# Attention with a window and global keys, then a gated feed-forward: the whole kernel written as one list of small steps

## The chip, the cores and the metric

The kernel runs on one core of a Trainium2 chip. A core has five engines that run side by side: TensorE (PE, matrix products), VectorE (DVE), ScalarE (ACT), GpSimd (POOL) and SyncE (SP, which here only issues transfers); each takes its instructions in order. PE writes to PSUM, which has eight banks of 512 float32 per partition; DVE and ACT can read them. Transfers from and to the chip's memory are issued from SP, ACT or POOL and carried by 16 DMA engines that all queues share. The metric is the device time of one execution in microseconds (us), given as the median of the runs; lower is better.

## The reference

Four batches, eight heads, 768 positions, 64 elements a head. A query sees the 8 first keys and the 96 keys up to itself, with a bias that falls with the distance. The result, 3072 rows of 512, goes through a feed-forward (FF) with a gate.

```python
scores = scale * np.matmul(q, k.transpose(0, 1, 3, 2))
is_global = pos[None, :] < 8
is_local = (rel >= 0) & (rel < 96)
dist = np.where(is_global & ~is_local, 96.0, np.abs(rel))
scores = np.where(is_global | is_local, scores - slopes[:, None, None] * dist, -1e9)
a = np.exp(scores - max); a = a / (np.sum(a, axis=-1) + 1e-09)
x = np.matmul(a, v)                         # -> (3072, 512)
g = x @ w_gate                              # (512, 1536)
out = (g / (1 + np.exp(-g))) * (x @ w_val) @ w_out
```

## The kernel before

Everything on PE is float16 with float32 sums. Tokens are worked in tiles of 384 (half a batch, eight tiles in all). The parts:

**Scores.** Keys are cut into seven chunks of 120 (the last has 48); each chunk's 128 columns of `kT` hold the 8 global keys and then the chunk's own. A chunk meets the 216 queries that can see it. Two heads (a pair, `hp`) lie in the upper and lower 64 rows of `qT` and `kT`, so that their score products run side by side. Two or three chunks share one PSUM bank of 432 columns; one such bank pair for two heads is what `scores` (line 357) or `scores_half` (line 338) makes. ACT takes the exponential of each head's bank (lines 351 and 375), and DVE or POOL multiplies it by `masks`, the exponential of the biased distance (lines 355, 383, 386). In the first half of batch 0, and a part of the second, the bias is instead added on PE by `bias` (line 327): a matmul of `slopeI`, the scaled unit matrix, with `dist`.

**Values.** A `Quad` is four heads. `weigh` (line 436, matmuls at 443) makes the denominators (`den`, with a matrix of ones) or one half of the numerators (`num`); four heads with 32 columns each run side by side. `invert` and `spread` (lines 450 and 457) make reciprocals on DVE with two transposes of 32x32 blocks, and the numerators, copied by ACT to `ns` (line 474), are scaled into `xT` by POOL (line 478), for batch 0 by DVE (lines 478, 499).

**Feed-forward.** For a tile t and one of 12 blocks f of 128 hidden units, `products` (line 506) makes four gate and four value matmuls of 384 columns. ACT takes a tanh (`th`, line 527), DVE makes `sl` (line 529) and `hT` (line 533), which must read a gate sum and then a value sum. `out_part` (line 537) makes a quarter of an output row block, three matmuls of 512 columns; after four, ACT evicts (`osb`, line 559) and SP stores.

**Order.** It is written by hand. At the start come warming matmuls (`fill`, 28 in all), then for each pair of batch 0 the transposes of the first half, the scores, the sums. Batch 0's V is loaded for its first half in rows of three tokens (`v16`), and `p_perm` (line 595) puts the rows in their key chunks with 12 matmuls with a 0/1 matrix `perm` (line 598), evicted by ACT and DVE (line 601). Then `stretches` (line 726) mix FF groups with attention steps: after every FF group a share `quota` is added to `owed`, and when it reaches 1 the next attention step is put in. What a step leaves for DVE or POOL waits in `later`. Each gate group is followed at once by the value group of the same f, and each output part by its place in `outs`. Loads are tied to places in the FF (`at_step`, line 737). Batch 0, and half of batch 1, are transposed on PE; the rest by transposing DMAs from SP (`transposes_dma`, line 394), after which `spread_keys` (line 403) copies the keys into their chunks on DVE.

**PSUM.** Eight single banks: `a0` to `a3` in turn for scores, sums and transposes (`bank`, line 236), `x0` to `x2` in turn for gate and value sums, `o0` for outputs.

**Loads.** POOL issues the casting loads (float32 to float16), SP the constants, the first two pairs of q and k in float32, the copies of the global values (`copy_globals`, line 183), the transposing DMAs and the stores.

Of the kernel before, what the change touches and what calls it, by code (L numbers as in the profile page):

```python
# [15 lines left out]
KC = 120  # L16
WIN = 216
# [18 lines left out]

@with_exitstack
def kernel(
# [31 lines left out]
    const_dr = nc.inline_tensor(  # L70
        np.concatenate([np.eye(128, 160, dtype=np.float16), dist_np], axis=1), name="consts")
# [23 lines left out]


    consts = sb.tile([128, 160 + 3 * WIN], FP16, name="consts")
    nc.sync.dma_start(out=consts, in_=const_dr.ap())
    identx, ident, dist = consts[:, 0:160], consts[:, 0:128], consts[:, 160:]


    J2 = TB // 128
    q32 = sb2.tile([128, H // 2, J2 * D], FP32, name="q32", tag="qst")
    k32 = sb2.tile([128, H // 2, J2 * D], FP32, name="k32", tag="kst")
    q16 = sb2.tile([128, 2, H, J2 * D], FP16, name="q16", tag="qst")
    k16 = sb2.tile([128, 2, H, J2 * D], FP16, name="k16", tag="kst")
    v16 = sb.tile([128, H, J2 * D], FP16, name="v16")
    for hp in range(2):
        for st, src in ((k32, k), (q32, q)):
            nc.sync.dma_start(  # L110
                out=st[:, 2 * hp:2 * hp + 2, :],
                in_=src[0, 2 * hp:2 * hp + 2, 0:TB, :].rearrange(
                    "h (p j) d -> p h (j d)", p=128))

    def load_half(dst, src, half, h0, h1):
        nc.gpsimd.dma_start(
            out=dst, in_=src[0, h0:h1, TB * half:TB * half + TB, :].rearrange(
                "h (p j) d -> p h (j d)", p=128))

    vSs = [sb.tile([128, NCH, H, D], FP16, name=f"vS{b}") for b in range(B)]  # L120
    for b in range(1, B):
        nc.gpsimd.memset(vSs[b][:, 6, :, :], 0.0)
    load_half(v16, v, 0, 0, H)
    load_half(k16[:, 0, 4:8], k, 0, 4, 8)
    load_half(q16[:, 0, 4:8], q, 0, 4, 8)

    masks = sb.tile([128, H, 3 * WIN], FP16, name="masks")
    ones = sb.tile([128, 256], FP16, name="ones")
    nc.vector.memset(ones, 1.0)

    NC0 = 4
    perm = sb.tile([128, J2, NC0, 128], FP16, name="perm")
    nc.vector.memset(perm.rearrange("p j c m -> p (j c m)").bitcast(mybir.dt.uint32), 0)
    kTs = [sb.tile([128, NCH * 128], FP16, name=f"kT{i}") for i in range(NP)]

    vS3 = sb.tile([128, H, D], FP16, name="vCut")


    nc.vector.memset(vSs[0][:, 6, :, :], 0.0)
    for t in kTs:  # L140
        nc.vector.memset(t[:, 3 * 128 + NG + TB - 3 * KC:4 * 128], 0.0)
        nc.vector.memset(t[:, 6 * 128 + 56:], 0.0)
    for j in range(J2):
        nc.vector.tensor_copy(
            out=perm[:, j, :, NG + j::J2],
            in_=identx.rearrange("p (c m) -> p c m", c=NC0))
        n = (NG - j + J2 - 1) // J2
        nc.vector.tensor_copy(
            out=perm[:, j, :, j:NG:J2],
            in_=identx[:, 0:n].unsqueeze(1).broadcast_to([128, NC0, n]))  # L150

    slopeI = sb.tile([128, H, 128], FP16, name="slopeI")

    def make_slope(eng, h):
        eng(slopeI[:, h, :], ident, -slopes[h] / scale)

    qst, kst = {}, {}

    def stage(b):
        qst[b] = sb2.tile([128, H, J * D], FP16, name="qst", tag="qst")  # L160
        kst[b] = sb2.tile([128, H, J * D], FP16, name="kst", tag="kst")

    def load_qk(b, h0, h1):
        for st, src in ((kst[b], k), (qst[b], q)):
            nc.gpsimd.dma_start(
                out=st[:, h0:h1, :],
                in_=src[b, h0:h1].rearrange("h (p j) d -> p h (j d)", p=128))

    def load_v_rest(b, c):
        n = min(KC, S - KC * c)  # L170
        nc.gpsimd.dma_start(  # L171
            out=vSs[b][NG:NG + n, c, :, :],
            in_=v[b, :, KC * c:KC * c + n, :].rearrange("h p d -> p h d"))


    vG = sb.tile([NG, B, H, D], FP16, name="vG")

    def load_globals():
        nc.gpsimd.dma_start(
            out=vG.rearrange("p b h d -> p (b h) d"),  # L180
            in_=v[:, :, 0:NG, :].rearrange("b h p d -> p (b h) d"))

    def copy_globals(b):
        c0 = 3 if b == 0 else 0
        nc.sync.dma_start(
            out=vSs[b][0:NG, c0:, :, :],
            in_=vG[:, b, :, :].unsqueeze(1).broadcast_to([NG, NCH - c0, H, D]))


    def stage_rows(b):  # L190
        qst[b] = sb2.tile([128, NP, J, 2, D], FP16, name="qst", tag="qst")
        kst[b] = sb2.tile([128, NP, J, 2, D], FP16, name="kst", tag="kst")

    def rows_of(st, b, hp):

        if b > 1:
            return st[b][:, hp]
        return st[b][:, 2 * hp:2 * hp + 2, :].rearrange("p h x -> p (h x)").rearrange(
            "p (t e d) -> p t e d", t=J, e=2)

    def load_rows(b, i, h):
        st, src = ((qst, q), (kst, k))[i]
        nc.gpsimd.dma_start(  # L203
            out=rows_of(st, b, h // 2)[:, :, h % 2, :],
            in_=src[b, h].rearrange("(t p) d -> p t d", p=128))

    wg = sb.tile([128, NC, DFF], FP16, name="wg")
    wv = sb.tile([128, NC, DFF], FP16, name="wv")
    wo = sb.tile([128, NFF, DM], FP16, name="wo")
    WF = 512  # L210

    def load_w(n, g):
        f0 = WF * n
        for w, src in ((wg, moe_w_gate), (wv, moe_w_val)):
            nc.gpsimd.dma_start(
                out=w[:, 2 * g:2 * g + 2, f0:f0 + WF],
                in_=src[256 * g:256 * g + 256, f0:f0 + WF].rearrange("(p s) f -> p s f", s=2))

    def load_wo(g):
        nc.gpsimd.dma_start(  # L220
            out=wo[:, 4 * g:4 * g + 4, :],
            in_=moe_w_out[512 * g:512 * g + 512].rearrange("(f p) d -> p f d", p=128))


    xTs = {}
# [5 lines left out]

    state = {"tags": ["a0", "a1", "a2", "a3"], "n": 0, "x": ["x0", "x1", "x2"]}

    def bank(name, dt=FP32):
        tag = state["tags"][state["n"] % len(state["tags"])]
        state["n"] += 1
        return single(name, tag, dt)

    def banks(name, dt=FP32):
        return [bank(name, dt) for _ in range(2)]

    def single(name, tag, dt=FP32):
        return ps.tile([128, 512 if dt == FP32 else 1024], dt, name=name, tag=tag)


    def make_masks(h, c0, c1):
        nc.scalar.activation(
            out=masks[:, h, c0:c1], in_=dist[:, c0:c1], func=AF.Exp, scale=-slopes[h])  # L250

    later = []

    def run_later(n):
        for _ in range(n):
            if later:
                later.pop(0)()

    class Pair:
        def __init__(self, b, hp):  # L260
            self.b, self.hp = b, hp
            self.at = {}

        def transposes(self):
            b, hp = self.b, self.hp
            trq, trk = (t[:, 0:S] for t in banks("trs", FP16))
            for st, tr in ((kst[b], trk), (qst[b], trq)):
                for j in range(J):
                    for hi in range(2):
                        nc.tensor.transpose(  # L270
                            tr[64 * hi:64 * hi + 64, 128 * j:128 * j + 128],
                            st[:, 2 * hp + hi, D * j:D * j + D], ident)
            self.qT = sb2.tile([128, S], FP16, name="qT", tag="qT", bufs=NP)
            self.kT = kTs[hp]
            k3 = self.kT.rearrange("r (c m) -> r c m", m=128)
            t3 = trk.rearrange("r (j p) -> r p j", j=J)
            for c0, c1, n in ((0, 6, KC), (6, 7, S - 6 * KC)):
                nc.scalar.copy(
                    out=k3[:, c0:c1, NG:NG + n].rearrange("r c (p j) -> r c p j", j=J),
                    in_=t3[:, 20 * c0:20 * c0 + (c1 - c0) * (n // J), :].rearrange(  # L280
                        "r (c p) j -> r c p j", c=c1 - c0))
            nc.scalar.copy(
                out=self.qT.rearrange("r (p j) -> r p j", j=J),
                in_=trq.rearrange("r (j p) -> r p j", j=J))
            nc.vector.tensor_copy(
                out=k3[:, :, 0:NG],
                in_=k3[:, 0, NG:2 * NG].unsqueeze(1).broadcast_to([128, NCH, NG]))


        def transposes_half(self, half, tr, k_eng):  # L290
            hp = self.hp
            trq, trk = tr
            for st, dst in ((k16, trk), (q16, trq)):
# [542 lines left out]
```

## Time and profile before

| what | value |
|---|---|
| median of three runs | 253.75 us (252.83 to 256.88) |
| the profiled execution, first to last instruction (its span; the profile gives no other time of it) | 252.9 us |
| PE busy | 241.3 us, 95% |
| DVE, ACT, POOL busy | 168.7, 130.9, 105.0 us |
| mean granted TensorE clock | 0.998 |
| DMA | 25.63 MB in 86499 packets, of which 76288 under 512 bytes |
| the chain that ended last | PE 80%, DVE 8%, ACT 4%, DMA 3% |

Busy times are from the profile's first part, of one execution. A group of instructions is given with its count, its busy time and the mean duration of one; PE's matmuls overlap, so that the distance from one start to the next, not the duration, is what one costs in a row. The chain that ended last is followed back from the last instruction, at each step to what released it.

### The profile page before, as it was taken

How to read it: one execution, taken by the hardware profiler on the slowest of the kernel's cores; microseconds unless marked ns; L12 is line 12 of the kernel's file. 1: busy time of each engine (PE TensorE's matmuls, PEld its weight loads, DVE VectorE, ACT ScalarE, POOL GpSimd, SP SyncE). 2: the span in 40 equal slices, each digit the busy share in tenths (PEclk: the TensorE clock that was granted, in tenths of full speed). 3: DMA queues.
4: the chain of work that ended last, by engine and by line, in shares of the span. 5: the costliest groups of instructions: out<-in, count | busy, mean ns of one | idle time of the engine just before them, and what ended most of it. 6: DMA issues, size and time to landing. Idle time of an engine off the chain costs nothing.

```text
span 252.9 us, 5999 instructions
## 1 busy us (share of the span) xinstructions
PE 241.3 (95%) x2384; PEld 136.1 (54%) x2384; DVE 168.7 (67%) x379; ACT 130.9 (52%) x290; POOL 105.0 (42%) x123
## 2 busy tenths in 40 slices
PE   6997999899889999999999999999999999999994
PEld 4664556464435556555555555555555555555541
DVE  7365779856695666979785656978875666555510
ACT  3476787559464455464653653555735634332321
POOL 9663664550054975913609865803020232200000
PEclk9999999999999999999999999999999999999999
DMA  6999999991950999993916997991011101100122
GB/s 157 188 203 181 180 207 205 167 131 42 127 69 4 141 150 173 129 143 64 117 44 67 150 157 88 147 109 45 0 44 41 44 0 44 43 20 24 41 83 83
DMA packets 86499, 25.63 MB, mean 101 GB/s; under 512 B 76288, under 2 KB 83528, under 8 KB 86472
## 3 DMA queue, kind: packets, MB, share of 16 engines
q0 software_dynamic: 65408, 13.83, 65.7%
q1 hardware_dynamic: 20920, 11.30, 21.8%
q8 instruction: 18, 0.29, 0.5%
q10 hardware_dynamic: 144, 0.13, 0.2%
q14 instruction: 9, 0.07, 0.1%
HBM read 28.63 MB, written 6.29 MB: 138 GB/s over the span
## 4 chain that ended last, share of the span: by engine, by line
PE 80%; DVE 8%; ACT 4%; DMA 3%; SPq 2%; issue 1%; DVEq 0%; ACTq 0%
PE ops L545 23%; PE gps L516 22%; PE vps L516 22%; PE num L443 3%; PE sc L366 2%; PE den L443 2%; DVE sl L529 2%; DMA kN<-kst 2%; DMA q<-in_q_dram 2%; ACT at L351 1%; PE trs L296 1%; PE warm L574 1%; PE sc L343 1%; PE psv L598 1%; SPq L399 1%
## 5 line engine op out<-in xcount | busy, mean ns | idle before, releaser
L529 DVE SCALAR_TENSOR_TENSOR sl<-th,gps 128x384 f32<-128x384 f32 x94 | 51.8, 552 | 45.4 <-ACT th L527 44.3
L527 ACT ACTIVATE th<-gps 128x384 f32<-128x384 f32 x94 | 46.4, 494 | 63.1 <-PE gps L516 61.6
L516 PE MATMUL gps<-xT,wg 128*128 128x384 f16 x376 | 77.0, 326 | 0.7 <-DVE xT L478 0.6
L516 PE MATMUL vps<-xT,wv 128*128 128x384 f16 x376 | 76.5, 326 | 0.5 <-DVE sl L529 0.4
L545 PE MATMUL ops<-wo,hT 128*128 128x512 f16 x288 | 75.5, 379 | 0.0
L533 DVE TENSOR_TENSOR hT<-vps,sl 128x384 f16<-128x384 f32 x94 | 51.7, 550 | 7.2
L478 POOL TENSOR_TENSOR xT<-ns,rb 128x384 f16<-128x384 f32 x24 | 23.9, 1013 | 77.5 <-DVE rb L459 62.4
L516 PEld LDWEIGHTS <-wg 128*128 128x128 f16 x384 | 35.8, 98 | 33.1 <-issue 3.1
L516 PEld LDWEIGHTS <-wv 128*128 128x128 f16 x384 | 36.8, 98 | 26.4 <-issue 2.1
L545 PEld LDWEIGHTS <-hT 128*128 128x128 f16 x288 | 27.4, 98 | 25.1 <-issue 0.4
L375 ACT ACTIVATE at<-sc 128x432 f16<-128x432 f32 x72 | 33.6, 535 | 9.0 <-PE sc L366 9.0
L171 POOL DMA_DIRECT2D vS<-in_v_dram x25 | 22.3, 898 | 9.1 <-DMA k<-in_k_dram 3.4
L559 ACT ACTIVATE osb<-ops 128x512 f32<-128x512 f32 x23 | 13.7, 597 | 18.0 <-PE ops L545 18.0
L474 ACT COPY ns<-num 128x384 f32<-128x384 f32 x28 | 12.0, 482 | 12.7 <-PE num L443 11.9
L203 POOL DMA_DIRECT2D qst<-in_q_dram x20 | 16.8, 854 | 2.7 <-DMA wo<-in_moe_w_out_dram 1.6
L203 POOL DMA_DIRECT2D kst<-in_k_dram x20 | 17.0, 865 | 2.0 <-DMA wo<-in_moe_w_out_dram 1.1
L386 DVE TENSOR_TENSOR at<-at,masks 128x864 f16<-128x864 f16 x20 | 12.9, 645 | 4.4 <-ACT at L375 4.4
L351 ACT ACTIVATE at<-sc 128x432 f16<-128x432 f32 (+2 forms) x32 | 11.5, 447 | 5.1 <-PE sc L343 5.1
L386 POOL TENSOR_TENSOR at<-at,masks 128x864 f16<-128x864 f16 x4 | 7.3, 1821 | 13.6 <-ACT at L375 13.6
L443 PE MATMUL num<-at,vS 128*32 128x216 f16 (+6 forms) x560 | 12.0, 226 | 0.0
L443 PE MATMUL den<-at,ones 128*32 128x216 f16 (+6 forms) x288 | 9.4, 229 | 2.4 <-DVE at L383 1.8
L443 PEld LDWEIGHTS <-ones 128*32 128x32 f16 x288 | 5.7, 96 | 9.2 <-issue 8.9
(76 smaller groups left out, 176.1 us busy)
## 6 DMA issues: line engine op xcount, KB each, us to landing
out_dram<-osb SPq DMA_DIRECT2D x23, 256.0 KB, 2.0
vS<-in_v_dram POOLq DMA_DIRECT2D x21, 120.0 KB, 8.1
kst<-in_k_dram POOLq DMA_DIRECT2D x20, 96.0 KB, 4.9
qst<-in_q_dram POOLq DMA_DIRECT2D x20, 96.0 KB, 4.7
wg<-in_moe_w_gate_dram POOLq DMA_DIRECT2D x6, 256.0 KB, 8.6
wv<-in_moe_w_val_dram POOLq DMA_DIRECT2D x6, 256.0 KB, 9.6
wo<-in_moe_w_out_dram POOLq DMA_DIRECT2D x3, 512.0 KB, 11.1
k<-in_k_dram SPq DMA_DIRECT2D x2, 192.0 KB, 3.8
```

The lines of the kernel that those rows point to most:

```text
L171: nc.gpsimd.dma_start(out=vSs[b][NG:NG + n, c, :, :], in_=v[b, :, KC * c:KC * c + n, :].rearrange("h p d -> p h d"))
L203: nc.gpsimd.dma_start(out=rows_of(st, b, h // 2)[:, :, h % 2, :], in_=src[b, h].rearrange("(t p) d -> p t d", p=128))
L351: nc.scalar.activation(out=at[:, hi, 0:col + n], in_=sc[hi][:, 0:col + n], func=AF.Exp, scale=scale)
L375: nc.scalar.activation(out=at[:, hi, :], in_=sc[hi][:, 0:BANK], func=AF.Exp, scale=scale)
L386: mul_eng.tensor_mul(at, at, m[:, :, o:o + BANK])
L443: nc.tensor.matmul(dst[r, o:o + n], lhsT=ones[:, 0:32] if side is None else vals[:, 4 * g + j, side::2], rhs=pairs[b, 2 * g + j // 2].at[c ...
L478: mul_eng.tensor_mul(self.x_out(half, side), srcs[side], self.rb)
L516: nc.tensor.matmul(gv[f, which][:, 0:TB], lhsT=w[:, c, 128 * f:128 * f + 128], rhs=x_of(t)[:, c, :], start=(c == 0), stop=(c == NC - 1))
L527: nc.scalar.activation(out=th, in_=dst[:, 0:TB], func=AF.Tanh, scale=0.5)
L529: nc.vector.scalar_tensor_tensor(out=sl, in0=th, scalar=1.0, in1=dst[:, 0:TB], op0=AluOp.add, op1=AluOp.mult)
L533: nc.vector.tensor_mul(hTs[t][:, f, :], dst[:, 0:TB], gv["sl"])
L545: nc.tensor.matmul(ops, lhsT=hTs[t][:, f, 128 * i:128 * i + 128], rhs=wo[:, f, :], start=(f == 0), stop=(f == NFF - 1))
```

## The change

The kernel's helpers become functions of small steps, and one text, `ORDER`, names every step once, in the order in which it is recorded (1,091 steps; each engine takes its own in that order). There is no `stretches`, `quota`, `owed`, `later`, `at_step`; a word such as `c.1.2.0` is the scores of batch 1, pair 2, unit 0, and a last letter V, A or P names the engine where it is open.

- **Steps.** Gate group (`g`), tanh (`t`), `sl` (`s`), value group (`v`) and `hT` (`h`) are separate, as are the score matmuls (`c`), their exponential (`x`) and mask (`m`), denominators and the two halves of numerators (`w`), and so on. The f of a tile come in any order; `sl` has five buffers and `th` three (two each before); exponentials' tiles have one more.
- **PSUM.** Two doubles (two banks each, `S0` and `S1`, in turn) for a pair's scores and for both halves of numerators; four singles for gate, value, output, transposes and denominators. A single is dealt in the order in which the list frees them.
- **One instruction for two.** The exponential of a pair's two heads is one ACT instruction on a double (864 elements for two of 432), and so is the copy of both numerator halves.
- **V straight.** `v16`, `perm`, `p_perm` and its evictions are gone: all seven chunks of batch 0's V come by `Lv` loads in key chunks, like those of the other batches. V has three buffers for the four batches.
- **Loads.** They stand in the list at their own places. Before the first weights come the first halves of q and k, four V chunks and the second halves of q and k of four heads. The two first q loads issue from ACT. The loads of q and k of batches 1 to 3 stand much earlier than their use. The constants come as two loads.
- **Which engine.** 21 of 40 mask steps are POOL's (4 of 52 mask instructions before), 14 of 32 scalings of numerators (24 before). In batch 0's second half pairs 0 and 1 take the bias on PE, pairs 2 and 3 masks.
- **The end.** The last 128 rows' sums go to the two banks of a double, in 24 matmuls of 256 columns (12 of 512 before), so that ACT and DVE each evict a bank of their own.

The core of the diff:

```diff
+ORDER = """
+pre Z.0.P Li fill.2 Lh.0.0.4.8 sl.2 sl.4 LG Lh.1.0.4.8 Lf.A.1.0 sl.7 fill.14 sl.6 cast.1.0.V T.0.0.1
+Lf.S.0.0 Lf.A.1.1 sl.1 sl.0 cast.0.0.V T.0.0.0 cast.1.1.A Lf.S.0.1 Lv.0.2 T.1.0.1 cast.0.1.A T.1.0.0
+Ld.S M.5.1 k.0.0.V B.0.1 q.0.0.V c.0.0.1 x.0.0.1 sl.3 B.0.0 c.0.0.0 M.4.0 Lh.1.1.0.4 x.0.0.0 q.1.0.V
+Lv.0.0 k.1.0.V G.0.1.4.V B.1.0 c.0.1.0 sl.5 T.2.0.1 T.2.0.0 k.2.0.V x.0.1.0 B.1.1 c.0.1.1 x.0.1.1
+T.3.0.0 q.2.0.A T.3.0.1 B.2.1 B.2.0 c.0.2.1 x.0.2.1 c.0.2.0 x.0.2.0 w.0.0.0.0 q.3.0.V B.3.0 k.3.0.V
+c.0.3.0 T.0.1.1 Lv.0.1 Lv.0.3 w.0.0.0.1 w.0.0.0.2 Lh.0.1.0.4 x.0.3.0 B.3.1 q.0.1.A c.0.3.1 Lw.0.0.0
+T.0.1.0 i.0.0.0 x.0.3.1 w.0.1.0.0 r.0.0.0 p.0.0.0.0.V Lw.0.0.1 k.0.1.A Lw.1.0.0 p.0.0.0.1.V Lw.1.0.1
+Lh.0.1.4.8 w.0.1.0.1 w.0.1.0.2 Lh.1.1.4.8 M.7.0 i.0.1.0 r.0.1.0 B.0.2 c.0.0.2 Lw.0.1.1 M.6.0
+Lw.0.1.0 Lv.0.6 Lw.1.1.0 T.1.1.1 q.1.1.A T.1.1.0 p.0.1.0.0.V ga.0.0 ga.0.2 p.0.1.0.1.V k.1.1.A g.0.3
...
+"""
...
+    def double(name, dt=FP32):
+        tag = f"S{turn['s'] % 2}"
+        turn["s"] += 1
+        return ps.tile([128, 2, 512 if dt == FP32 else 1024], dt, name=name, tag=tag)
+    busy = {tag: None for tag in XT}
+    freed = list(XT)
+    def single(name, key, dt=FP32):
+        tag = freed.pop(0)
+        busy[key] = tag
+        return named(name, tag, dt)
+    def release(key):
+        freed.append(busy.pop(key))
...
+    def ld_v(b, c):
         n = min(KC, S - KC * c)
         nc.gpsimd.dma_start(
-            out=vSs[b][NG:NG + n, c, :, :],
+            out=v_of(b)[NG:NG + n, c, :, :],
             in_=v[b, :, KC * c:KC * c + n, :].rearrange("h p d -> p h d"))
...
+        nc.scalar.activation(
+            out=at[:, :, 0:w], in_=scs.pop((b, hp, u))[:, :, 0:w], func=AF.Exp, scale=scale)
...
+            if last_rows(t, i):
+                for e in range(2):
+                    c = slice(DM // 2 * e, DM // 2 * e + DM // 2)
+                    nc.tensor.matmul(ops[:, e, 0:DM // 2], lhsT=lhsT, rhs=wo[:, f, c],
+                                     start=(f == 0), stop=(f == NFF - 1))
...
-    def p_perm(c, eng):
-        psv = p_single("psv", "v")
-        for j in range(J2):
-            nc.tensor.matmul(
-                psv, lhsT=perm[:, j, c, :], rhs=v16[:, :, D * j:D * j + D],
-                start=(j == 0), stop=(j == J2 - 1))
...
+    for step in ORDER.split():
+        name, *args = step.split(".")
+        WORK[name](*(int(a) if a.isdigit() else a for a in args))
```

## The prediction

> **What bounds the kernel now.** I read the shares first, then the windows, then the chain of waits, then single stretches of the timeline.
>
> ```profile
> span 252.9 us, 5999 instructions
> PE 241.3 (95%) x2384; PEld 136.1 (54%) x2384; DVE 168.7 (67%) x379; ACT 130.9 (52%) x290; POOL 105.0 (42%) x123
> ...
> DMA  6999999991950999993916997991011101100122
> ```
>
> TensorE (PE) sets the time; every digit of the DMA row is one fortieth of the span, and the transfers are full up to about 57 us. But a busy PE is not PE at its peak. The chain of waits gives the pitch of matmuls that follow one another:
>
> ```profile
> 79.94 1.29 PE ops L545 x6
> 81.23 0.65 PE gps L516 x4
> ```
>
> Six matmuls of 512 columns take 1.29 us and four of 384 take 0.65: 0.42 ns a column. At that pitch the whole work is 192 groups x 0.65 = 124.8 (gate and value) + 288 x 0.215 = 61.9 (output) + 8.8 (scores, two heads side by side) + 13.2 (denominators and numerators, four side by side) + 2.9 (bias) + 3.9 (transposes) + 2.6 (V permutation) = 218. I call that the pipelined work; 35 us of the span are not that. Counting each window's matmuls at that pitch shows where they are.
>
> ```profile
> core 0: us, PE busy (x) PEld busy (x) DVE busy (x) ACT busy (x) POOL busy (x), PEclk, DMA share, GB/s
> 20.00:30.00 10.00, 8.93 (x117) 5.34 (x118) 7.80 (x19) 6.09 (x15) 4.38 (x6) 1.00 1.63 184
> 30.00:40.00 10.00, 9.58 (x154) 5.89 (x149) 7.34 (x20) 8.48 (x23) 6.47 (x9) 1.00 1.28 205
> 40.00:50.00 10.00, 9.15 (x114) 5.22 (x113) 8.84 (x19) 6.64 (x19) 4.41 (x6) 1.00 1.67 186
> 60.00:80.00 20.00, 17.86 (x193) 9.38 (x191) 15.23 (x36) 11.16 (x25) 4.60 (x5) 1.00 0.53 76
> 80.00:100.00 20.00, 20.00 (x234) 11.36 (x236) 13.25 (x28) 9.96 (x21) 15.80 (x20) 1.00 1.66 132
> ```
>
> In 20-30, for one, 16 + 12 gate and 8 value matmuls (0.1625 each) are 5.85, transposes, scores and sums 1.8: 7.65. So counted, the pipelined work is 1.4 in 0-10, 6.5 in 10-20, 23.5 in the 30 us from 20 to 50 (6.5 lost), 15.4 in 60-80 (4.6 lost), then 154 in the 160 us to 240 (6 lost); the end loses 4. So the loss is the start (12 us before the feed-forward, FF), the first FF tile beside batch 0's second half, and batch 1's first half.
>
> ```profile
> 10.90 1.29 PE psv L598 x6
> ...
> 13.09 1.40 PE psv L598 x6
> ...
> 23.29 0.81 PE gvps L516 x4
> ```
>
> The start is one chain through load, casts, scores, exponentials, denominators, with V's permutation (psv) in PE's order between them; the first gate product that continues comes at 22.8. In the trace the first weight blocks land at 13.5 to 18.2 us, the second at 25.0 to 28.9, the third at 33.4 to 37.2: the start is bound by order, not by weights.
>
> **The change part by part.** Sum against the execution of 252.9 us; the median of the runs is 253.75, 0.85 more.
>
> *Start.* V in key chunks takes away 12 psv matmuls (12 x 0.224 = 2.7 us on PE), four evictions (0.6 to 0.7 each) and 0.7 + 1.5 us of permutation building on DVE; fills fall from 28 to 16. Exponentials of two heads become one instruction: 535 ns at 432 and 323 at 168 elements give 0.8 ns an element over 0.19 fixed, so 0.88 for 864 in place of 0.95 for two in a row. V chunks cost 0.93 us of transfer each (landings at 29.87 and 30.83), four before the weights = 3.7, where the one load of V's half took 1.5; two half-1 loads of 1.0 to 1.4 also stand ahead of the weights. So 18.2 becomes about 22 for the value block and 18.5 to 19 for the gate block, which now goes first (wg before wv). Two q loads issue from ACT (0.5 each, before its table load), which SP no longer issues. DVE has 12 to 13 us to do from the first landing near 4, so x is ready at 17 to 19; the second numerators' double waits for DVE's first xT products inside that. The first gate starts near 19.5, not 22.8 (3.3), with 7.7 us of pipelined work behind it, not 6.0 without psv (1.7). Bounds: 0 if the loads are late by 4, 6 if they are as before. **-4.5.**
>
> *First FF tile.* The list keeps gate groups ahead of value groups (five sl buffers), and puts batch 0's half 1 into the weight gaps. From 10 to 31 us of PE work DVE has 41 instructions, 20.7 us at their pitch (two xT in 1.01); third-block weights land near 33 to 36 by the same landing steps (1.3 a block), when PE asks for them at about 32. DVE, 99% as long as PE's 21, is next: I take 24.5 us for these 21, 3.5 lost in place of 6.5. Bounds: nothing gained, or all but DVE's own 0.5. **-3.1.**
>
> *Batch 1.* The kst/qst of the first two head pairs land at 46.7 and 48.7 now; the new load order puts them ahead of part of wo, near 40 to 42. Transposes and scores then lie among tile 1's groups, with output parts kept back as cover. In 60-80 the chain runs through kN (DMA 4.3 us), kT and masks. I take 1.2 of 4.6 left; bounds 0 and 4.6. **-3.4.** The transposes share SP's queue with the output stores; a late transpose holds the store behind it, and with two osb buffers ACT's third eviction.
>
> *Later.* PSUM: doubles carry scores and numerators, four singles the rest. 21 masks move to POOL (1.82 each there, 0.61 on DVE), ten xT products from POOL (1.01) to DVE (0.55). Bias grows by 672 columns (+0.3). The last 128 rows go as 24 matmuls of 256 columns (fills at full pace: 0.127 each, 3.05 against 2.58, +0.5), and ACT and DVE then empty two banks together (-0.4). Cost of POOL's tensor work on DVE: the timeline has it.
>
> ```profile
> 65.19 0.17 DVE L410 COPY kT<-kN 128x48 f16<-128x48 f16 x1
> ...
> 69.28 2.12 POOL L478 TENSOR_TENSOR xT<-ns,rb 128x384 f16<-128x384 f32 x2 [15.11 <-ACT at L375]
> ...
> 69.48 0.98 DVE L410 COPY kT<-kN 128x48 f16<-128x48 f16 x1
> ...
> 70.46 1.40 DVE L386 TENSOR_TENSOR at<-at,masks 128x864 f16<-128x864 f16 x1
> ```
>
> The same copy takes 0.17 alone and 0.98 beside POOL, a mask 1.40 for 0.60. FF's own sl and hT do not change (552 ns both ways). Bounds 0 to 7; I take 0.9, since DVE has a third of its time free. **+1.3 in all.**
>
> Sum: -4.5 - 3.1 - 3.4 + 1.3 = -9.7; 252.9 - 9.7 = 243.2, as a median **244.0**.
>
> The busy share would allow less. PE idles 2.3 us in 20-50 and 2.1 in 60-80, so by that row the two middle terms could give at most 4.4, not 6.5, and the time would be 246. The Trainium skill ("Perfetto Trace Analysis", section "Identifying the Most-Contended Engine") says matmul busy share is a bad measure of headroom, because matmuls are pipelined; by that rule the time is 244, and this trace's pitches agree.
>
> **The rivals.**
> 1. *Transfers hold the start* (0.10): first FF no earlier than 22.8 and later blocks late too. For: DMA is full, and V's rows are now 256-byte runs. Against: the weights land 4 us before their use now. Start 0, first tile -2: 249.6, within 2%.
> 2. *POOL holds up DVE* (0.08): 35 tensor instructions, 52 us of POOL in some 180, meet 54 key copies and masks on DVE; 0.29 x 54 = 16 hits of 0.8 = 12.6 us of DVE. If half lies where DVE is the limit, +6.3 in place of 0.9: 249.4. The Trainium skill ("SBUF — State Buffer", section "Who interferes with whom") says that a DVE instruction with two SBUF inputs contends with GpSimd's reads and that 2-port copies are locked out whole; by that rule more POOL masks mean this case, and the two rows above agree.
> 3. *Singles run out* (0.12), slower: gate, value, output, denominator and transpose sums share four banks. An output part holds one for four parts; three banks turn in 3 x 0.65 = 1.95 us. A gate bank is held 0.65 + 0.49 + 0.55 = 1.69, and 2.57 when its tanh stands behind a merged exp of 0.88: 0.62 lost. 44 exps lie beside FF: 27 us if each hits. It makes the kernel slower from 24 of 44 (15 us); at two thirds, 262. Against: three banks serve gate and value now, exps come in pairs of 0.95, and 80-240 loses only 6 in 160.
>
> **How the numbers follow.** Forecast 0.70, rivals 0.10, 0.08, 0.12. A measurement here tells about 2% from no change, 248.7 to 258.8. Faster 0.72 (the forecast and the better edge of rivals 1 and 2), within 2% 0.16, slower 0.12. The range: all favourable bounds together (-6, -6, -4.6, +0.3) give 237; upward it takes in rivals 1 and 2: 238 to 252.
>
> **What would show it.** Right: psv gone, first gate before 21 us; windows from 22 to 80 with 9 or more us of pipelined work in 10; DVE over 80% in the first tile; steady part unchanged. Wrong: gate matmuls waiting for weight landings (1); masks and kT copies near 1 us on DVE with PE waiting for them (2); many gate groups in 80-240 ended by sl or th (3). PE idle over 3 us between 5 and 19 us would slow its matmuls (fills: 0.225 each at 6.7 us, 0.127 at 10) and cost 2 to 3.

## The result and the profile after

The changed kernel takes **264.04 us** (median of 4 runs, 262.62 to 266.10) against 253.38 (4 runs, 252.83 to 256.88) for the kernel before on the same chip: a ratio of **1.041, 95% interval 1.036 to 1.045**. It is slower, where 244.0 was forecast and 0.12 was given to slower. The execution in the profile took 266.1, with a span of 263.9. All ratios in this text leave out executions more than 1.5% above the fastest of their kernel (medians and ranges keep them), and the profiles of runs 1, 6 and 12 below are of such executions, so that what only they show is not settled.

The page of the changed kernel, with the row of the clock that TensorE was granted (each digit is a fortieth of the span, 6.6 us, in tenths of full speed):

```profile
span 263.9 us, 5821 instructions
PE 242.0 (92%) x2368; PEld 136.0 (52%) x2368; DVE 168.5 (64%) x364; ACT 119.6 (45%) x216; POOL 130.4 (49%) x142
...
PEclk9689999999779999999599999999999999999999
DMA  7999969999997999990152996610014011101212
```

The sums hardly moved: DVE is as busy as before, ACT 11 us less, POOL 25 us more. But the clock row, all nines before, has three dips, at 7 to 20, 66 to 79 and 125 to 132 us; and the DMA row has a dip at 33 to 40 and then hardly a rest up to 119, where the kernel before was quiet at 57 to 63 and at 70 to 82. The windows say which stretches lost time:

```profile
core 0: us, PE busy (x) PEld busy (x) DVE busy (x) ACT busy (x) POOL busy (x), PEclk, DMA share, GB/s
20.00:30.00 10.00, 10.00 (x127) 5.99 (x124) 8.51 (x21) 8.06 (x18) 5.74 (x10) 1.00 1.49 195
30.00:40.00 10.00, 9.89 (x158) 6.06 (x157) 9.33 (x19) 7.14 (x15) 9.14 (x12) 1.00 0.79 113
60.00:80.00 20.00, 13.80 (x133) 6.47 (x135) 10.33 (x27) 6.23 (x10) 11.23 (x13) 0.83 2.03 141
120.00:130.00 10.00, 5.17 (x20) 2.17 (x21) 7.23 (x8) 0.42 (x2) 4.65 (x4) 0.71 0.00 0
```

Read the matmul counts: 133 in 60-80 where there were 193, and 20 in 120-130. With each matmul at its pitch, as in the prediction, the time that is not pipelined work (fills and the V permutation left out of the work) is:

| stretch | before, lost us | after, lost us | change | forecast |
|---|---|---|---|---|
| to the first gate group (22.8; 20.56) | 16.15 | 13.38 | -2.8 | -4.5 |
| from there to 60 | 5.51 | 3.10 | -2.4 | -3.1 |
| 60 to 80 | 4.57 | 10.25 | +5.7 | -3.4 |
| 80 to 110 | 1.69 | 4.38 | +2.7 | the three: +1.3 |
| 110 to 130 | 1.07 | 8.15 | +7.1 | |
| 130 to the end | 7.50 | 7.93 | +0.4 | |

These add up to +10.7; with 0.3 more work that is the 11.0 between the two spans. So at 60 us the changed kernel is 5.2 us ahead, at 80 it has lost that, and 10 us more go by 130. The waits of PE (us in total, times, longest):

```profile
PE sc L471 <- DVE kT L437: 6.6, 2, 5.2
PE sc L471 <- DMA qT<-qst: 4.3, 1, 4.3
PE num L530 <- DMA vS<-in_v_dram: 2.5, 2, 1.5
```

POOL's timeline shows both of the causes that the runs below bear out:

```profile
29.76 2.61 POOL L498 TENSOR_TENSOR at<-at,masks 128x144 f16<-128x144 f16 x4 [2.31 <-ACT at L481]
33.23 1.82 POOL L498 TENSOR_TENSOR at<-at,masks 128x864 f16<-128x864 f16 x1 [0.86 <-ACT at L481]
34.99 0.81 POOL L289 DMA_DIRECT2D qst<-in_q_dram  x1
...
115.32 9.33 POOL L498 TENSOR_TENSOR at<-at,masks 128x864 f16<-128x864 f16 x7
```

**The stop near 120.** From 115.32 on POOL runs seven masks without a pause. DVE's timeline beside them:

```profile
117.06 0.56 DVE L592 TENSOR_TENSOR hT<-vps,sl 128x384 f16<-128x384 f32 x1 [0.28 <-PE vps L576]
117.53 5.45 DVE L434 COPY kT<-kN 128x720 f16<-128x720 f16 x1
122.91 1.78 DVE L436 COPY kT<-kN 128x48 f16<-128x48 f16 x1
```

A key copy that takes 0.34 us alone starts during the second mask and takes 5.45; the next, 0.17 alone, takes 1.78 and ends with the row. Everything on DVE waits behind them, and PE stands from 119.62 to 124.83.

**The stop near 68.** The first three lines of POOL's timeline: three mask steps of batch 0 stand ahead of batch 1's loads in its queue, and POOL issues no load between 26.74 and 34.99. The rest is in the chain that ended last (start, us, what):

```profile
54.77 8.76 DMA qst<-in_q_dram
...
63.67 7.87 DMA qT<-qst
...
75.16 1.28 PE ops L610 x3
...
78.33 1.29 PE ops L610 x6
```

The last rows of head 5's queries are issued at 54.77 and land at 63.53; their transposition takes another 7.87, and PE stands from 67.31 to 71.59. The last two lines are the same output matmuls: 0.43 us each after the stop, 0.215 three us later. After the stop at 120 nine of them take 4.05 us from 126.92 on (PE's timeline):

```profile
124.83 0.90 PE L471 MATMUL sc<-qT,kT 64*128 64x216 f16 x8 [5.21 <-DVE kT L437]
125.66 1.46 PE L576 MATMUL vps<-xT,wv 128*128 128x384 f16 x4
126.92 4.05 PE L610 MATMUL ops<-wo,hT 128*128 128x512 f16 x9
```

That is 2.1 more than at full pace; the scores and value matmuls ahead of them lost another 1. So these two stops cost their length and 2.5 to 3 us behind it.

### The profile page after: what moved, and what is told of

Same layout as the page of the kernel before. It is cut to its first block, busy times and chain, and to the rows that moved or that the text cites. A ratio compares the mean times of both kernels' runs of the same rounds, so it can differ in the third digit from the quotient of the medians.

```text
span 263.9 us, 5821 instructions
## 1 busy us (share of the span) xinstructions
PE 242.0 (92%) x2368; PEld 136.0 (52%) x2368; DVE 168.5 (64%) x364; ACT 119.6 (45%) x216; POOL 130.4 (49%) x142
## 4 chain that ended last, share of the span: by engine, by line
PE 74%; DMA 13%; DVE 6%; POOL 4%; issue 1%; ACT 1%; SPq 0%; ACTq 0%; POOLq 0%
PE vps L576 21%; PE gps L576 20%; PE ops L610 18%; PE sc L471 5%; DMA qst<-in_q_dram 3%; DMA qT<-qst 3%; PE num L530 3%; POOL qst L300 2%; DMA vS<-in_v_dram 2%; DMA k<-in_k_dram 2%; DMA kN<-kst 2%; DVE kT L434 2%; PE sc L458 2%; PE den L530 2%; PE trs L361 1%; DVE at L498 1%
## 5 line engine op out<-in xcount | busy, mean ns | idle before, releaser
L610 PE MATMUL ops<-wo,hT 128*128 128x512 f16 x276 | 70.7, 393 | 0.0
L498 POOL TENSOR_TENSOR at<-at,masks 128x864 f16<-128x864 f16 (+3 forms) x29 | 38.5, 1357 | 27.0 <-ACT at L481 18.8
L481 ACT ACTIVATE at<-sc 128x864 f16<-128x864 f32 (+2 forms) x52 | 42.2, 834 | 20.6 <-PE sc L471 20.5
L562 POOL TENSOR_TENSOR xT<-ns,rb 128x384 f16<-128x384 f32 x14 | 15.4, 1111 | 45.8 <-DVE rb L552 27.9
L259 POOL DMA_DIRECT2D vS<-in_v_dram x28 | 25.4, 912 | 4.1 <-DMA wo<-in_moe_w_out_dram 1.7
L471 PE MATMUL sc<-qT,kT 64*128 64x216 f16 (+4 forms) x240 | 16.0, 251 | 10.8 <-DVE kT L437 6.6
L471 PEld LDWEIGHTS <-kT 64*128 64x128 f16 x240 | 8.6, 97 | 21.2 <-issue 8.5
L498 DVE TENSOR_TENSOR at<-at,masks 128x864 f16<-128x864 f16 (+1 forms) x25 | 14.0, 583 | 1.3 <-ACT at L481 1.3
L539 ACT COPY ns<-num 128x768 f32<-128x768 f32 x12 | 9.6, 798 | 11.6 <-PE num L530 11.6
L434 DVE COPY kT<-kN 128x720 f16<-128x720 f16 x10 | 9.2, 920 | 6.5 <-DMA kN<-kst 6.5
```

The lines of the kernel that those rows point to most:

```text
L259: nc.gpsimd.dma_start(out=v_of(b)[NG:NG + n, c, :, :], in_=v[b, :, KC * c:KC * c + n, :].rearrange("h p d -> p h d"))
L471: nc.tensor.matmul(sc[:, hi, col:col + n], lhsT=kTs[hp][r, 128 * c:128 * c + 128], rhs=qTs[b, hp][r, q0:q0 + n], start=fresh, stop=True, s ...
L481: nc.scalar.activation(out=at[:, :, 0:w], in_=scs.pop((b, hp, u))[:, :, 0:w], func=AF.Exp, scale=scale)
L498: ENG[e].tensor_mul(a2, a2, m[:, :, m0:m0 + n])
L562: ENG[e].tensor_mul(x_of(2 * b + half)[:, 2 * g + side, :], nums[b, g, half][:, side, 0:TB], rbs[b, g, half])
L610: nc.tensor.matmul(ops, lhsT=lhsT, rhs=wo[:, f, :], start=(f == 0), stop=(f == NFF - 1))
```

## The experiments

Three theories were on record. **A**: POOL's masks do the harm, in two ways: in POOL's queue they hold up loads (first half), and beside DVE they hold up its key copies (second half). **B**: transfers that nobody needs yet stand ahead of those that are due. **C**: the list's order is tight on DVE, whatever runs on POOL. Each result is a median with its ratio to the kernel before in the same comparison.

**1. All POOL masks on DVE.**

```diff
-m.0.3.2.P m.0.2.2.P ... m.3.3.2.P
+m.0.3.2.V m.0.2.2.V ... m.3.3.2.V
```

> All 21 mask steps that the list gives to POOL go to DVE, at the same places in the list; nothing else changes. Theory A (POOL's masks do the harm: in POOL's queue they hold up the loads behind them, and on the shared way to SBUF they hold up DVE's key copies): the gap without loads on POOL from 27.5 to 35.0 us closes, the key copy that took 5.45 us takes about 0.35, PE's losses fall from 10.2 to about 5 us in 60-80 and from 7.3 to about 1 in 120-130; DVE has 21 x 0.6 = 13 us more work, which costs 1 to 2. Time 252 (250 to 255). Theory B (the transfers issued early for batches 2 and 3 fill the queues and delay batch 1's rows and the transposing transfers; the masks' engine does not matter): 263 to 266. Theory C (PE simply takes its list in an order that waits, and DVE is nearly full): 264 to 270, DVE being the busier.

Measured 259.26, ratio 1.019 (1.011 to 1.026): 4.8 us below the changed kernel, where A expected 12. The stop at 120 is gone; in 60-80 of its profiled execution, 9.9 us are still lost.

**2. Only batch 0's three masks on DVE** (`m.0.3.2`, `m.0.2.2`, `m.0.3.3`).

> Only batch 0's three mask steps go from POOL to DVE. Theory A, its first half (masks stand ahead of loads in POOL's queue): the q and k loads of batch 1 and wo issue from 28 us and not from 35, the last rows of q for pair 2 land before 60 and not at 63.5, and PE's loss in 60-80 falls by about 5; the stop near 118-125 stays. Time 259 (257 to 261). Theory B: 264, since the same transfers only start earlier and still lie ahead of batch 1's last rows. Theory C: 264 to 265.

Measured 260.57, ratio 1.026 (1.016 to 1.035). The waits of PE (these kernels' lines are 8 lower):

```profile
PE sc L463 <- DVE kT L429: 6.8, 2, 5.2
PE sc L463 <- DMA qT<-qst: 1.9, 1, 1.9
```

Batch 1's first load is issued at 27.82 and the last query rows of head 5 land at 59.47, 4 us sooner; the stop at 68 shrinks to 1.9, and 60-80 loses 3.3. The stop of 5.2 stays, as A has it.

**3. The other 18 masks on DVE**, batch 0's left on POOL.

> The 18 mask steps of batches 1 to 3 go from POOL to DVE; batch 0's three stay on POOL. Theory A, its second half (POOL's masks in a row keep DVE's key copy from starting): no key copy over 1 us, PE's loss in 120-130 falls from 7.3 to about 1, that in 60-80 stays near 10. Time 257 (255 to 259). Theories B and C: 263 to 266, with the stop near 118-125 still there for another reason.

Measured 262.37, ratio 1.033 (1.028 to 1.038), not 257. The stop at 120 is gone, but new waits for masks that are now late on DVE (4.0 us in all, up to 1.4 each) give much of it back. So C is true of DVE's masks: the list has no room there for 18 more.

**4. The three key copies of each pair on ACT, masks as they are.**

```diff
     def spread_keys(b, hp):
-        nc.vector.tensor_copy(
+        nc.scalar.copy(
```

> The three copies that put the keys of a pair in their chunks after a transposing transfer (10 pairs) go from DVE to ACT; all masks stay where they are. If POOL's masks keep DVE from its way to SBUF, the copies on ACT take the same time beside POOL as without it (about 0.8, 0.2 and 0.2 us), the stop near 118-125 is gone although POOL's seven masks in a row stay, and the time is 257 (255 to 259) with 12 us more of ACT work at 45% busy. If the stop comes from the transfers or from the list's order, it stays: 263 to 266.

Measured 257.46, ratio 1.015 (1.008 to 1.022), as A expected. POOL's timeline:

```profile
109.86 9.23 POOL L498 TENSOR_TENSOR at<-at,masks 128x864 f16<-128x864 f16 x7
```

ACT's timeline beside it:

```profile
115.44 0.78 ACT L434 COPY kT<-kN 128x720 f16<-128x720 f16 x1
```

The row of seven is there and as long as ever; the copy beside it takes 0.78 on ACT. 110-130 loses 0.8 instead of 8.15. So the harm is the meeting of that row with DVE's copy. (Moving the copies also takes 13 us of work off DVE; run 11 breaks the row and leaves them there.)

**5. The loads in another order**, engines as in the changed kernel: batch 1's rows ahead of the output weights, most V chunks and batch 2's rows.

```diff
-L4.1.0 Lo.0 L4.0.0 Lo.1 Lr.1.0.7 Lv.1.0 Lr.1.1.7 Lr.1.0.4 ... Lo.2 Lr.2.1.2 Lr.2.0.7 Lr.1.1.4 ...
+L4.1.0 L4.0.0 Lr.1.0.4 Lr.1.0.5 Lr.1.1.4 Lr.1.1.5 Lo.0 Lv.1.0 Lr.1.0.6 ... Lo.1 Lv.1.3 Lv.1.1 Lo.2
```

> Only the order of loads is edited: on POOL's queue batch 1's staged heads and rows go ahead of the output weights, of most V chunks and of batch 2's rows, and the four transposing DMAs of batch 1's pairs 2 and 3 go to SP together, ahead of the first tile of batch 1 by TensorE. Batch 0's masks stay on POOL and ahead of all of these loads, and the key copies stay on DVE. Theory A as first written (batch 0's masks hold the loads): the loads still start near 35 us, so the stop of 4.3 us at 67 stays for the most part: 262 to 265. Theory B (the rows of heads 4 and 5 are put behind loads that nobody needs yet, and their transposition then shares the DMA engines with those): the query rows land near 50 instead of 63.5, qT of pair 2 is there before 60, and 60 to 80 us loses some 4 us instead of 10.2: about 258. Both leave the stop near 120 (5.2 us) in place.

Measured 264.54, ratio 1.039 (1.032 to 1.047). The number is A's, the reason is not. The waits of PE:

```profile
PE ops L610 <- DMA wo<-in_moe_w_out_dram: 8.3, 2, 5.5
PE sc L471 <- DVE kT L437: 6.8, 2, 5.2
```

The wait for qT is gone, and PE waits for the output weights instead, which now come last. The stop only changed hands.

**6. Edits 2 and 4 together.**

> Two edits that were tried one at a time are put together: batch 0's three POOL masks on DVE, and the key copies on ACT; all other masks stay on POOL. If the two stops have two separate causes (masks ahead of loads in POOL's queue; masks holding DVE's key copies), the gains add: 264.0 less 3.5 less 6.6 is about 254. If both work through one shared slack (theory C: the list's order is tight on DVE and the end is set elsewhere), the second adds little: 257 to 258.

Measured 255.51 (10 runs, 252.01 to 258.35), ratio 1.003 (0.999 to 1.006): by the medians 8.5 us off the changed kernel, of the 3.5 + 6.6 = 10.1 that two causes in full would give. By the ratios the two edits take off 3.8%, and one at a time 1.5% and 2.6%. So the gains nearly add, as two separate causes would have it. In its profiled execution (257.05) the loads start at 28.25 and the query rows land at 59.91, yet the transposition took 8.89 and PE stood 5.5 us for it. There, getting the loads issued sooner was not enough.

**7. Edits 2, 4 and 5 together.**

> The two edits before together with the order of loads of the first (batch 1's rows ahead of the output weights and batch 2's rows, the four transposing DMAs issued together). If all the loss of 60 to 80 us beyond before's 4.6 is the late query rows and the slow transposition, 60 to 80 loses 2 to 4 us, and the time is 248 to 251, below the kernel before. If the transposing DMAs are slow whatever goes ahead of them (7 to 9 us each, one behind the other), the stop only moves, and it is 253 or more.

Measured 256.91, ratio 1.011 (1.006 to 1.015): not the 248 to 251 of the first case but the 253 or more of the second. The first transpositions of batch 1 took 10.3 and 12.1 us, and a stop of 4.4 us, waiting for the output weights, stands in place of that for qT.

**8. The kernel before, with the masks of batches 2 and 3 on POOL.**

```diff
-        on_vector = b < 2 or bk < 2 or hp % 2 == 0
+        on_vector = b < 2
```

> The kernel before with one edit: the masks of batches 2 and 3 on POOL (24 instead of 4), everything else as it was; the key copies stay on DVE. Theory A, second half (POOL's masks in a row hold DVE's two-byte copies of the keys, whatever the kernel): key copies of several us and stops of TensorE behind them, 3 to 10 us in all, so 256 to 263. Theory C (it is the new list's order that is tight): DVE loses some 10 us of work, and the time stays at 252 to 255.

Measured 258.15, ratio 1.017 (1.012 to 1.022): in A's range, but not by A's stops. The waits of PE:

```profile
PE den L443 <- POOL at L383: 2.8, 5, 0.7
PE den L443 <- DVE at L383: 1.4, 2, 0.7
```

PE waits a little, often, for masks that POOL finishes late; the longest key copy is 0.99 us, since here no copy falls beside a row of masks, and the longest row is three. So the masks cost the kernel before 4.5 us too, in part by coming late. What a long row does to a copy is not tested by this run.

**9. Loads by need**, with edits 2 and 4: the first two loads of the output weights where they were, then the rows of heads 4 and 5, the third load of the output weights (issued at 37.1 us, in run 6 at 46.2), V chunks, heads 6 and 7, the four transpositions of batch 1 together, and batch 2's rows last.

```diff
-... Lr.1.0.7 Lv.1.0 Lr.1.1.7 Lr.1.0.4 Lr.1.0.5 Lr.1.0.6 ... Lo.2 Lr.2.1.2 Lr.2.0.7 Lr.1.1.4 Lr.1.1.6 Lr.1.1.5
+... Lr.1.0.4 Lr.1.0.5 Lr.1.1.4 Lr.1.1.5 Lo.2 Lv.1.0 Lv.1.3 Lv.1.1 Lr.1.0.6 ... Lv.1.2 ... Lr.2.1.2 Lr.2.0.7
```

> Batch 0's masks on DVE and the key copies on ACT as in the run that joined these two, and the loads of 35 to 65 us in the order in which TensorE comes to need them: batch 1's first four heads and the output weights as they were, then the rows of heads 4 and 5 and their two transposing DMAs, then V chunks 0, 3 and 1, then the rows of heads 6 and 7, batch 2's rows last. Theory B (what comes late is late because other loads stand ahead of it on the same DMA engines; with wo first it was the query rows, with the rows first it was wo): both in time, 60 to 80 us loses 3 to 5 us instead of 9.4, and the time is 249 to 252. If the DMA engines can't carry all that is wanted by 65 us in any order, a stop of 3 to 5 us stays, on wo, on V or on qT, and it is 254 to 257.

Measured **252.17** (10 runs, 250.67 to 253.98), ratio **0.994 (0.991 to 0.998)**: 12 us below the changed kernel and a little below the kernel before, though within the 2%. 60-80 loses 4.2 us, as B said. The transposition of pair 2's queries still took 8.78 us, but it was issued at 46.9, not 63.7: it had to be early more than short.

**10. Two thirds of the output weights' loads left out**, on the kernel of run 6.

```diff
-Lo.1
-Lo.2
-                nc.tensor.matmul(ops, lhsT=lhsT, rhs=wo[:, f, :],
+                nc.tensor.matmul(ops, lhsT=lhsT, rhs=wo[:, f % 4, :],
```

> As the run with batch 0's masks on DVE and the key copies on ACT, with the load order of the changed kernel, but only the first third of the output weights is loaded (two of three loads, 2 MB read and 1 MB written, are left out) and the output projections all read that third; TensorE's work is the same. Theory B (the DMA engines, full from 8 to 65 us, set the stop at 63 to 69): about 6 us of transfers less, the query rows land 5 to 6 us earlier, the stop goes, and the time is 249 to 251. If the stop comes from the transposing DMAs' own length (7 to 9 us) or from the place of the scores in the list, it stays at 4 us or more: 254 to 256.

Measured 249.57, ratio 0.983 (0.976 to 0.991): 5.9 us below run 6 by the medians, 2% (5 us) by the ratios. The window 60 to 80 of run 9 (columns as above):

```profile
60.00:80.00 20.00, 17.69 (x207) 9.55 (x200) 13.70 (x27) 11.46 (x19) 14.99 (x17) 1.00 1.64 148
```

The same window of run 10:

```profile
60.00:80.00 20.00, 20.00 (x224) 11.05 (x222) 14.78 (x32) 14.06 (x25) 14.96 (x17) 1.00 1.60 136
```

207 and 224 matmuls in place of 133. In 10 the transposition of the queries took 4.41 us, and no stop is left there: with fewer loads ahead, everything that 60 to 80 needs is in time. B holds for the first stop. Whether it is the bytes or the two places in POOL's queue of loads that count, run 10 does not separate; run 9 gets most of the way with all bytes, by order.

**11. Three masks of the row on DVE** (five of its seven instructions), all else as in the changed kernel.

```diff
-m.2.1.1.P ... m.2.2.1.P ... m.2.2.0.P
+m.2.1.1.V ... m.2.2.1.V ... m.2.2.0.V
```

> The changed kernel with 3 of its 21 POOL masks on DVE: units 1 of pairs 1 and 2 and unit 0 of pair 2 of batch 2, which are five of the seven instructions that POOL runs in a row at 115 to 125 us. If the harm is the row (a key copy on DVE waits until POOL pauses), the copy near 117 takes under 2.5 us instead of 5.45 and the stop of 5.2 us falls to 2 or less: 258 to 260. If it is POOL's tensor work as such, spread over batches 1 to 3, three masks of 21 bring a seventh of the 6.6 us that moving the copies brought: about 263.

Measured 258.51, ratio 1.018 (1.012 to 1.024): three letters bring 5.5 us. POOL's timeline:

```profile
115.04 3.64 POOL L498 TENSOR_TENSOR at<-at,masks 128x864 f16<-128x864 f16 x2
```

DVE's timeline beside it:

```profile
117.25 1.65 DVE L434 COPY kT<-kN 128x720 f16<-128x720 f16 x1
118.82 0.17 DVE L436 COPY kT<-kN 128x48 f16<-128x48 f16 x1
```

The copy meets only the last mask; that ends at 118.68, and the copy at 118.90; the next copy runs alone, at its 0.17. The stop at 120 is gone.

**12. The order by need carried on to batch 2.** Batch 2's first pairs ahead, V chunks 4 to 6 of batch 1 earlier, batch 3 last, and pair 1's key transposition ahead of pair 2's.

> The run with the loads in the order of need, with the same thought carried on to 65 to 110 us: of batch 2's rows those of its first two pairs first, batch 1's V chunks 4 to 6 ahead of batch 2's, batch 3's rows behind all of batch 2's, and the transposing DMA and the key copies of pair 1 of batch 2 ahead of those of pair 2, whose scores come later in the list. Theory B (order of transfers): the stops at 86.8 us (0.97, a V chunk) and 95.0 us (1.84, key copies behind a transposition that landed at 94.3) go, 80 to 110 loses 3 us instead of 5.9, and the time is 249 to 250.5. If the order there costs nothing (the stops only move on), 251.5 to 253.

Measured 254.22 (12 runs), ratio 0.999 (0.996 to 1.002): a miss, 2 us worse than 9. In its profiled execution (255.87), three transpositions go to SP together, at 86.92, 88.43 and 90.41, take 9 us each, and PE stands 4.9 us for the last. There, the two stops it was made for became one longer one.

## Why the prediction was wrong

**The start and the first FF tile** were right in kind and too large: -2.8 and -2.4 of -4.5 and -3.1. (The two parts that the forecast names for the start, 3.3 and 1.7, add up to 5.0; it took 4.5.) The first gate group comes in at 20.56, not 19.5. The weights land a little sooner than they were put (gate at 17.85, value at 20.41), but PE stood 2.3 us for the first transposes' keys, and the clock was halved from 8.07 to 14.90 (granted 0.76 in 10-20). The forecast put that slowing behind an idle of over 3 us. 20-50 loses 2.9 us where 3.5 was said, with DVE 85, 93 and 88% busy.

**Batch 1** (-3.4) is the first step that failed: +5.7. The forecast followed the first two pairs alone; these land at 39.8 (queries) and 46.0 (keys), where 40 to 42 was said. Pairs 2 and 3 come by rows and transpositions, and the query rows of heads 4 to 6 stand behind the output weights and two rows of batch 2. Their transposition was taken to cost what it cost before, where it had the DMA engines almost to itself; now the loads that the change issues early run beside it, and each takes two to three times as long. The trace of the kernel before had such lengths too, a little further on: 7.00, 7.88 and 8.53 us for those issued from 88.4 to 92.2, beside batch 2's loads. They cost little there (80 to 110 loses 1.69), and the forecast did not use them. The note that transpositions share SP's queue looked at the stores and not at POOL's loads. Rival 1 had the right resource and looked for it 40 us too early, at the first weights.

**Later** (+1.3, in it 0.9 for POOL beside DVE) is the second: +10.2. Rival 2 had the mechanism, POOL holding up DVE. Its price, +6.3, is near what the runs show (6.6 us when the copies leave DVE, 5.5 when the one row is broken), but by luck: it was the half of 16 hits of 0.8 spread over the kernel, and what came was one copy held for 5.45. The rival was given 0.08, and the forecast took 0.9, because each meeting was priced at the 0.8 us that a copy loses beside one POOL instruction, and spread over DVE's free third. The list has masks in rows of up to seven instructions: the copy waits for the row, not for one instruction, and what waits behind it on DVE is the feed-forward itself. The list, which was at hand, shows that row; it was counted but not read.

The Trainium skill ("SBUF — State Buffer", section "Who interferes with whom") says that whoever has the shared ports keeps them for a whole instruction, and that ACT never waits. The second agrees with run 4 (0.78 on ACT). The first is less than what is seen: after the copy's start four changes from one POOL instruction to the next go by (118.1 to 120.9), and only at the fifth, at 122.7, does a copy of 0.34 us get through. Here the measurement decides.

**Singles run out** (rival 3) didn't happen: no gate group appears among PE's waits, and from 130 on the loss is 7.9 against 7.5.

The two waits for V chunks and keys in 80 to 110 (+2.7) look like late transfers too, but no run brought the loss of that stretch near the 1.69 of before (it is 3.9 to 8.2 us in every run of the changed kernel; in run 12 the wait for V went and a longer one for queries came), so their cause is only argued. Nor is it settled why runs 1 and 6, whose loads start as early as run 2's, still stood 4.8 and 5.5 us for qT in their profiled executions. Head 5's query rows landed at 61.2 and 59.9 there (59.5 in run 2), and the transposition took 8.46 and 8.89 (7.21).

## What to carry to other kernels

When loads are moved ahead of their use, ask of every transfer that is due in that stretch what now runs beside it: its length is not the one it had in a quiet queue, and what is put first makes something else last (qT, then wo, then batch 2's keys). When work moves to POOL, read its queue for two things: which loads stand behind it, and whether its tensor instructions form a row next to a two-byte copy on DVE; a row can cost the copy nearly all of its length, and ACT can take such copies. And price a stop of TensorE of some 2 us or more with the half pace that may follow it.

## What the runs showed of the hardware that was not expected

- **A DVE copy can wait almost to the end of a row of POOL masks**: 0.34 us became 5.45 in a row of seven (so in the changed kernel and run 2; 5.46 in run 5), 1.65 beside the last of a row of two. It is not so of every row: at 160.43 in the changed kernel such a copy passed in 0.35, where one of POOL's scalings gave way to the next. Why the changes between masks let nothing by is open. FF's own `sl` and `hT` took 0.55 us through it all, and POOL's row was 9.33 long with DVE's copy beside it and 9.23 without.
- **The clock after a stop.** Stops of 4.27 and 5.21 us were followed by matmuls at half pace (nine output matmuls in 4.05 us, 0.43 each from one start to the next, after the second); the stop of 1.9 us in run 2 left the granted clock at 1.00. The Trainium skill ("TensorE: Matmul & The Clock Gate", section "What's actually happening") has the clock halve after an idle window of about 3.4 us. The traces fit the window's length, but the stop may be shorter: 2.29 us up to 8.18 in the changed kernel and 1.84 us up to 96.82 in run 9 were followed by half clock too (granted 0.50 from 8.07 to 14.90, and from 98.07 to 101.48). In the traces' record, the moments at which the clock changes lie whole multiples of 3.41 us apart (in the changed kernel it falls at 8.07, 69.51 and 124.13). Cut at these multiples, the 14 traces hold 957 windows that began at full clock: the 20 with over 1.8 us without a matmul were all followed by half clock, and none of the 920 with under 1.39 was. So it matters where a stop falls among these windows, not only how long it is.
- **The transposing DMA's length, from issue to landing, goes with what else is in flight**: 2.8 to 4.3 us in the kernel before at 62 to 69 us, 7.0 to 8.5 there and 7.9 to 9.2 in the changed kernel beside POOL's loads, 12.2 and 12.5 in run 5, 4.4 in run 10.
- **POOL's loads are at most eight deep, as this program is built.** From the ninth on, each waits until the one eight places ahead has landed: landings at 44.00, 45.96 and 48.55, issues at 44.29, 46.24 and 48.84. In the trace these loads use eight semaphores in turn, each waiting for its own, so this is the program's limit; what the chip would allow, no run shows. A load late in the list can't start early, however idle POOL is.
